# Holding full-array TensorE work back until the next step's projections are placed

## The chip, the cores and the metric

The kernel runs on one core of a Trainium2 chip. The metric is the device time of one execution in microseconds, of which each kernel got several. All executions quoted here ran fast (granted TensorE clock 0.98 to 0.99 over the span).

In the profile's lines PE is TensorE (matmuls), ACT is ScalarE, DVE is VectorE, POOL is GpSimd and SP is SyncE, which issues the DMA transposes. L753 is line 753 of the kernel. An *eviction* is the copy by ACT or DVE that takes a matmul's result out of its accumulator (`pb`) into SBUF. A *landing* is the time from the issue of a transfer to its arrival.

## The reference

Four blocks follow one another, each with a residual and a layernorm: A, B, A, B. Block A is a recurrence of 64 steps ("segments") of 32 tokens with 8 memory tokens. Block B is a linear attention without recurrence.

```python
def _A_ref(x, mem0, Wq, Wk, Wv, Wo, seg_len):   # x 1x2048x512, 32 heads of 128, M = 8, seg_len = 32
    mem = mem0
    for s in range(n_seg):
        h = jnp.concatenate([mem, xs], axis=1)          # xs: the segment's 32 tokens
        q, k, v = (einsum('btd,dhe->bhte', h, W) for W in (Wq, Wk, Wv))
        ...                                             # mask, softmax
        o = jnp.einsum('bhqk,bhke->bhqe', p, v)
        o = jnp.einsum('bhte,hed->btd', o, Wo)
        mem = o[:, :M, :].copy()                        # the next step needs this
        outs.append(o[:, M:, :])
...
x = x + _A_ref(_layernorm(x), ...)
x = x + _B_ref(_layernorm(x), B_wqkv, B_wo)
x = x + _A_ref(_layernorm(x), ...)
x = x + _B_ref(_layernorm(x), B_wqkv, B_wo)
```

The chain from step to step is: memory rows of h, projections, scores and attention of the memory rows, output projection, "next memory" (the selection of the 8 memory rows, transposed), and the projections again.

## The kernel before

The kernel is a program that builds its own instruction order. Each piece of work becomes a node with a cost, an engine, a mode ("col" for TensorE's 32-column tiles, "full" for the whole array) and a priority from the table OFFSET. A list schedule then places the nodes at build time. The token-only part of h (the "left-over" rows, one block of projections for each group of four steps) and block B's work serve as filler beside the recurrence. "x scores" are the attention scores of the token rows, "x sums" the sums of their softmax.

```python
def turned(W, key, blk, bkeys, b, dst, dkey, urgent, dma):   # q or k, half b, turned so that e is on partitions
    tl = project(W, key, blk, bkeys, b, urgent)              # 16 column-tile matmuls of 512 columns
    ...
    nd = evac(img[:, k, :], lambda: tl.f32()[:, :], 512, ...)
    if dma:                                                  # half 0 of q and k, and the left-over block
        add("sp", lambda e: e.dma_start_transpose(dst.rearrange("p h j x -> p h (j x)"), img[:, k, :]), 1.25, ...)
        return nd
    ...                                                      # half 1: 16 transposes on TensorE, then an eviction
def sums(pe):                                                # x sums, full array
    o = tl.f32()[:, 256:512].rearrange("p (h q) -> p h q", h=8)
    pe.matmul(o, bo_sb[:, :], Px[:, :, :], start=True, stop=False)
    return pe.matmul(o[:, :, 0:8], bo_sb[:, :], PLL[:, g2, :, gl], start=False, stop=True)
def next_mem(s, w):                                          # full array, one matmul for each half
    ...
            return pe.matmul(tl.f32()[:, 16 * h:16 * h + 16], outW[:, w, 128 * h:128 * h + 128], selm_sb[:, :],
                             start=True, stop=True)
        add("pe", mm, 0.13, reads=[("outW", w, h), "selm"], tiles=[tl], urgent=True)
...
for i in range(4):                                           # output weights in four parts
    ... s.dma_start(Wo_sb[:, hs, :], wo_view[:, hs, :]) ... after=[late[-2]]
    late.append(nd)
```

`late` holds the weight loads in order, so the second part of Wo waits for Wv, the third for the first part, the fourth for the second.

The softmax here doesn't subtract the row's maximum and nothing guards it: scores larger than these inputs give would overflow.

Of the kernel before, what the change touches and what calls it, by code (L numbers as in the profile page):

```python
# [18 lines left out]
TURN = 1.8  # L19
MODE_SLACK = 13.03  # L20

LOOK = 0.073

PERIOD = 13.5
OFFSET = {
    "ld0": (0.05,),
    "ld1": (7.40,),
    "ld2": (2.50,),
    "ld3": (-5.00,),
    "ld4": (0.50,),  # L30
    "startF": (-0.15,),
    "prepF": (9.60, 3.45, -2.05, 2.25, -11.65, 7.20, 10.15, 0.00, 0.25, -2.25, 10.95),
    "left0F": (-6.25, -5.55, -4.70, 8.10, 1.10, 5.50),
    "left1F": (-3.35, 2.30, 1.95, 0.40, 0.00, 0.00),
    "leftv0F": (10.40, -13.80),
    "leftv1F": (-3.30, 4.80),
    "leftsF": (18.35, 1.45, 0.00, 1.00),
    "xl": (-5.85,),
    "qk0": (-12.95, -6.45, 8.05, -4.60, -13.05, 0.00),
    "qk1": (-0.20, 0.35, 5.25, -8.40, 2.50, -2.40, 9.25, -8.65),  # L40
    "v0": (-0.55, -0.90),
    "v1": (8.80, -1.35),
    "mem0": (0.00, -13.00, -2.00, -17.55, -26.85, -27.15, -14.75, -2.10, -0.90),
    "mem1": (4.25, 0.00, -7.80, -23.75, -16.20, 5.95, 6.50, -7.85, -17.95),
    "out": (2.10, -0.45, -23.15, 0.05),
    "next": (-1.20, 7.90, -0.75),
    "x": (7.25, 0.90, 0.00, 9.35, 8.55, -9.50, 8.35, -18.15, -6.05, 43.75, -2.50, 3.20, -4.50, -1.00, 4.50,
        -8.10, 0.00, 20.70, 27.10, -7.10, 25.80, -2.00, 1.60),
    "res": (44.00, 3.50, -3.65, 4.65, -11.50, 0.50, -0.15),
    "prep": (-11.65, -5.70, 0.00, -1.20, -0.30, -4.45, 0.60, -12.75, -15.65, -8.55, -12.05),  # L50
    "left0": (-4.05, 9.15, 3.55, -11.25, -2.45, 3.55),
    "left1": (0.40, 1.35, -3.70, 27.15, 1.10, -1.45),
    "leftv0": (29.25, 0.25),
    "leftv1": (16.10, 3.05),
    "lefts": (12.95, -2.65, 3.45, 0.45),
    "bi": (1.10, -0.95, 2.45, -8.45, -3.70, -13.50, -7.60, -0.80, -0.75, 14.70, 9.05, -1.60, 5.90, -2.85,
        19.95, 3.55, 4.65, -6.75, -1.20, -4.45, -6.25, 13.60, -15.25),
    "xL": (6.15, 14.85, 0.00, -0.65, 8.15, -18.50, 0.00, 16.95, -6.95, 8.65, -10.95, -11.15, -0.50, 7.10, 0.25,
        2.45, 4.85, -3.40, -1.55, 1.25, 0.70, 1.85, -5.55),
    "outL": (2.90, -6.30, 2.15, -13.50),  # L60
    "resL": (3.05, 0.10, 30.35, 1.95, -12.55, 5.05, 2.05),
    "biL": (-10.20, -13.70, -30.55, -9.65, 5.20, -12.00, -1.55, -6.15, 10.10, 2.55, 0.20, 5.15, 23.35, -10.60,
        21.70, 1.35, -2.40, 7.10, -1.40, -11.85, 4.30, 17.05, 4.30),
    "bm": (0.40, -22.15, -6.45, -6.75, -9.40, 14.30, 1.65, -9.70, 10.35, 3.65, -33.85, 15.75, -5.20),
    "boF": (-5.65, 9.70, -18.05, -1.25, 20.15, -8.70, -6.00, 8.15),
    "bo": (4.10, -23.70, 4.30, 5.10, -10.15, -3.90, -2.35, 0.00),
    "boL": (3.10, 0.90, -3.25, 4.45, -6.85, 2.75, -11.45, 28.45, -4.85),
}
# [35 lines left out]
class _Node:  # L104
    __slots__ = ("engs", "fn", "cost", "sync", "order", "tiles", "dsem", "dval", "eng", "start", "done",
                 "tail", "sig", "val", "waits", "know", "idx", "succ", "nleft", "urgent", "mode", "prio", "lat", "soft", "key")


class _Prog:
# [27 lines left out]
    def add(self, engs, fn, cost, reads=(), writes=(), tiles=(), dsem=None, urgent=False, mode="full",  # L137
# [3 lines left out]
        nd.lat = lat  # L141
        nd.key = None
        if self.place is not None:
            step, name = self.place
            nd.key = (step, name, self.count)
            self.count += 1
# [43 lines left out]
    def schedule(self):  # L190
# [90 lines left out]
        EPS = 0.03  # L281

        def pick_for(e):
            tn = self.now[e]
# [6 lines left out]
            while ready[e]:  # L291
                item = heapq.heappop(ready[e])
                nd = item[2]
                if nd.done is not None:
                    continue
                if first_of(nd):
# [34 lines left out]
        while n_left:  # L331
# [7 lines left out]
            if pick is None:  # L339
                ev = [t for t in self.now.values() if t > t_low + 1e-9]  # L340
                for e in ENGINES:
                    if pend[e]:
                        ev.append(pend[e][0][0])
                for own in self.bank_owner:
                    if own is not None and own.ops[-1].done is not None:
                        ev.append(own.ops[-1].done + PE_LAG)
                        ev.append(own.ops[-1].done + HOP)
                nxt = [t for t in ev if t > t_low + 1e-9]
                if not nxt:
                    raise RuntimeError("scheduler stuck: %d left" % n_left)  # L350
                t = min(nxt)
                for e in ENGINES:
                    if self.now[e] < t:
                        self.now[e] = t
                continue
# [19 lines left out]
            if e == "pe":  # L375
                if nd.mode != self.pe_mode:
                    nd.start += PE_SWITCH
                self.pe_mode = nd.mode
            nd.done = nd.start + nd.cost[e] + nd.lat
            self.now[e] = nd.start + nd.cost[e] - (0.09 if e == "act" else 0.05 if e == "dve" else 0.0)  # L380
# [94 lines left out]
def _build_kernel(nc, A_x, A_mem0, A_Wq, A_Wk, A_Wv, A_Wo, A_seg_len, B_wqkv, B_wo, out):  # L475
# [144 lines left out]
    late = []  # L620
    for i, (W, v, nm, t) in enumerate(((Wq_sb, qk_view[0], "Wq", 12.4), (Wk_sb, qk_view[1], "Wk", 22.0),
                                       (Wv_sb, qk_view[2], "Wv", 31.0))):
        P.at(-9000 + 1000 * i, "ld%d" % (2 + i))
# [3 lines left out]
    for i in range(4):  # L627
        hs = slice(8 * i, 8 * i + 8)
        nd = add("sp", lambda s, hs=hs: s.dma_start(Wo_sb[:, hs, :], wo_view[:, hs, :]), 0.9, writes=[("Wo", i)],
                 dsem="dWo%d" % i, after=[late[-2]], lat=(12.4, 5.6, 5.7, 5.8)[i])  # L630
        late.append(nd)
    add("sp", lambda s: s.dma_start(wqkv_sb[:, :, :], B_wqkv.rearrange("(c p) f -> p c f", p=128)), 0.5,
        writes=["wqkv"], dsem="dwqkv", after=[late[-1]], lat=5.0)
    late.append(P.nodes[-1])
# [103 lines left out]
    def a_layer(base, first):  # L738
        def at(s, name):

            P.at(base + s, name + ("F" if s < 0 else "L" if s >= NSEG or (s == NSEG - 1 and name == "x") else ""))


        def project(W, key, blk, bkeys, b, urgent):
            tl = P.tile()
            for c in range(4):
# [3 lines left out]
                def mm(pe, c=c):  # L750
# [4 lines left out]
                    return r  # L755
                add("pe", mm, c_pe4(4, 512), reads=[key] + bkeys, tiles=[tl], urgent=urgent, mode="col")
            return tl
# [25 lines left out]
        def left_block(G, step):  # L783
# [3 lines left out]
            for b in range(2):  # L787
                at(step, "left%d" % b)
                hs = slice(4 * b, 4 * b + 4)
                turned(Wq_sb, "Wq", blk, bk, b, qTl[:, r2, hs, :, :], ("qTl", r2, b), False, True)  # L790
                turned(Wk_sb, "Wk", blk, bk, b, kTl[:, r2, hs, :, :], ("kTl", r2, b), False, True)
            for b in range(2):
# [83 lines left out]
        def x_attention(s):  # L876
# [25 lines left out]
            def sums(pe):  # L902
                o = tl.f32()[:, 256:512].rearrange("p (h q) -> p h q", h=8)
                pe.matmul(o, bo_sb[:, :], Px[:, :, :], start=True, stop=False)
                return pe.matmul(o[:, :, 0:8], bo_sb[:, :], PLL[:, g2, :, gl], start=False, stop=True)
            add("pe", sums, c_pe(1, 256) + c_pe(1, 64), reads=["Px", ("PLL", g2), "bo"], tiles=[tl])
            add("act", lambda a: a.activation(Rx[:, :, :].rearrange("p h q -> p (h q)"), tl.f32()[:, 256:512], ACTF.Ln),
# [29 lines left out]

        def out_proj(oT, keys, urgent):

# [3 lines left out]
            for hh in range(8):  # L943
# [3 lines left out]
                def mm(pe, hh=hh):  # L947
# [7 lines left out]
                    return r  # L955
                add("pe", mm, 2 * c_pe4(4, 256), reads=[("Wo", i) for i in range(4)] + keys[hh // 4], tiles=[tl],
                    urgent=urgent, mode="col")
            for h in range(2):
# [5 lines left out]
        def out_block(s):  # L964
            at(s, "out")
            keys = [[("oTm", s % NO, b), ("oTx", s % NO, b)] for b in range(2)]
            return out_proj(oTb[:, s % NO, :, :], keys, True)

        def next_mem(s, w):
# [3 lines left out]
            for h in range(2):  # L973
                def mm(pe, h=h):
                    return pe.matmul(tl.f32()[:, 16 * h:16 * h + 16], outW[:, w, 128 * h:128 * h + 128], selm_sb[:, :],  # L975
                                     start=True, stop=True)
                add("pe", mm, 0.13, reads=[("outW", w, h), "selm"], tiles=[tl], urgent=True)
            evac(hT[:, G1 % 2, g1, :, 0:8].rearrange("p (d h) m -> p h d m", d=2),
# [53 lines left out]
        for s in range(NSEG):  # L1032
# [6 lines left out]
            for b in range(2):  # L1039
                at(s, "qk%d" % b)  # L1040
                hs = slice(4 * b, 4 * b + 4)
                turned(Wq_sb, "Wq", blk, bk, b, qT[:, r2, hs, :, :], ("qT", r2, b), True, QDMA[b])
                turned(Wk_sb, "Wk", blk, bk, b, kT[:, r2, hs, :, :], ("kT", r2, b), True, KDMA[b])
            for b in range(2):
# [206 lines left out]
```

## Time and profile before

| | us |
|---|---|
| median of 3 runs (range) | 1869.79 (1865.63 to 1869.96) |
| span of the profiled run | 1867.5 |
| first next memory | 60.7 |
| 62 steps of layer 1 / of layer 2 | 831.3 / 841.5 |
| jump between the layers / tail | 67.5 / 66.6 |

The table's cut at the first matmul of next memory in each step is the prediction's. The page's views are read in the prediction. It uses PE's wait list only in part, so here are its first rows for 56 steps of layer 1 (100 to 860 us). A row gives the waiting line, what ended the wait, the total in us, the number of waits and the longest.

```profile
PE pb L775 <- ACT arena_sb L591: 4.6, 7, 1.2
PE pb L803 <- DMA arena_sb<-arena_sb: 2.6, 3, 0.9
PE pb L775 <- DVE arena_sb L592: 2.5, 4, 1.0
PE pb L753 <- DVE arena_sb L592: 2.3, 14, 0.2
PE pb L837 <- DMA arena_sb<-arena_sb: 1.4, 3, 0.8
```

### The profile page before, as it was taken

How to read it: one execution, taken by the hardware profiler on the slowest of the kernel's cores; microseconds unless marked ns; L12 is line 12 of the kernel's file. 1: busy time of each engine (PE TensorE's matmuls, PEld its weight loads, DVE VectorE, ACT ScalarE, POOL GpSimd, SP SyncE). 2: the span in 40 equal slices, each digit the busy share in tenths (PEclk: the TensorE clock that was granted, in tenths of full speed). 3: DMA queues.
4: the chain of work that ended last, by engine and by line, in shares of the span. 5: the costliest groups of instructions: out<-in, count | busy, mean ns of one | idle time of the engine just before them, and what ended most of it. 6: DMA issues, size and time to landing. Idle time of an engine off the chain costs nothing.

```text
span 1867.5 us, 95161 instructions
## 1 busy us (share of the span) xinstructions
PE 1762.9 (94%) x43796; PEld 1201.8 (64%) x43905; DVE 1065.5 (57%) x3267; ACT 1160.3 (62%) x3015; POOL 74.5 (4%) x172
## 2 busy tenths in 40 slices
PE   4899999999999999999799999999999999999996
PEld 1566767666666667676456666766667666676662
DVE  1455555656565565655445556556555665565555
ACT  2466666666666666666456666666666666666655
POOL 2000000000000000000000000000000000000000
PEclk8999999999999999999899999999999999999999
DMA  9512121221222121211021222122122221212213
GB/s 336 126 35 42 35 43 37 43 40 37 43 37 43 35 46 37 45 38 40 21 42 35 42 38 48 40 37 45 37 44 42 45 43 38 45 38 54 45 34 124
DMA packets 228256, 96.86 MB, mean 52 GB/s; under 512 B 211624, under 2 KB 222000, under 8 KB 226320
## 3 DMA queue, kind: packets, MB, share of 16 engines
q1 hardware_dynamic: 220656, 62.58, 18.1%
q0 software_dynamic: 5616, 15.60, 2.7%
q10 hardware_dynamic: 1584, 12.58, 1.7%
q8 instruction: 343, 5.62, 1.3%
q14 instruction: 57, 0.47, 0.1%
HBM read 29.89 MB, written 10.49 MB: 22 GB/s over the span
## 4 chain that ended last, share of the span: by engine, by line
PE 85%; DMA 10%; ACT 2%; DVE 2%; issue 1%; SPq 0%; ACTq 0%; DVEq 0%
PE pb L753 39%; PE pb L952 15%; DMA arena_sb<-arena_sb 8%; PE pb L928 4%; PE pb L837 3%; PE pb L775 3%; PE pb L993 3%; PE pb L1088 2%; PE pb L975 2%; PE pb L854 2%; PE pb L892 2%; PE pb L1124 1%; PE pb L868 1%; PE pb L1190 1%; PE pb L867 1%
## 5 line engine op out<-in xcount | busy, mean ns | idle before, releaser
L591 ACT ACTIVATE arena_sb<-pb 128x512 bf16<-128x512 f32 (+6 forms) x1309 | 682.0, 530 | 341.5 <-PE pb L753 272.5
L753 PE MATMUL pb<-Wk_sb,arena_sb 128*32 128x512 bf16 x5120 | 347.7, 383 | 5.5 <-DMA Wk_sb<-in_A_Wk_dram 5.5
L753 PE MATMUL pb<-Wv_sb,arena_sb 128*32 128x512 bf16 x5120 | 352.2, 381 | 0.0
L753 PE MATMUL pb<-Wq_sb,arena_sb 128*32 128x512 bf16 x5120 | 342.2, 383 | 5.4 <-DVE arena_sb L592 4.8
L952 PE MATMUL pb<-Wo_sb,arena_sb 128*32 128x256 bf16 x10368 | 312.3, 275 | 4.9 <-DMA Wo_sb<-in_A_Wo_dram 2.9
L592 DVE CAST arena_sb<-pb 128x128 bf16<-128x128 f32 (+3 forms) x452 | 179.9, 398 | 221.3 <-PE pb L975 110.0
L952 PEld LDWEIGHTS pb<-Wo_sb,arena_sb 128*32 128x32 bf16 x10368 | 274.2, 97 | 20.7 <-DMA Wo_sb<-in_A_Wo_dram 3.4
L913 DVE TENSOR_TENSOR arena_sb<-arena_sb 32x256 bf16<-32x256 bf16 x512 | 212.1, 414 | 50.9 <-ACT arena_sb L909 38.8
L592 DVE COPY arena_sb<-pb 128x512 bf16<-128x512 bf16 (+2 forms) x325 | 121.2, 380 | 191.6 <-PE pb L775 183.9
L753 PEld LDWEIGHTS pb<-Wk_sb,arena_sb 128*32 128x32 bf16 x5120 | 136.9, 97 | 133.6 <-DMA Wk_sb<-in_A_Wk_dram 5.6
L753 PEld LDWEIGHTS pb<-Wq_sb,arena_sb 128*32 128x32 bf16 x5120 | 124.2, 96 | 111.3 <-DVE arena_sb L592 10.6
L753 PEld LDWEIGHTS pb<-Wv_sb,arena_sb 128*32 128x32 bf16 x5120 | 132.5, 97 | 98.1 <-issue 2.8
L591 ACT ACTIVATE outW_sb<-pb 128x128 fp32r<-128x128 f32 x228 | 63.2, 277 | 200.0 <-PE pb L952 198.0
L775 PEld LDWEIGHTS pb<-id_sb,arena_sb 128*32 128x32 bf16 x4096 | 76.4, 96 | 95.0 <-ACT arena_sb L591 47.5
L775 PE MATMUL pb<-id_sb,arena_sb 128*32 128x128 bf16 x4096 | 103.1, 220 | 24.1 <-ACT arena_sb L591 20.2
L928 PE MATMUL pb<-arena_sb 128*128 128x128 bf16 x1024 | 118.7, 217 | 5.5 <-DVE arena_sb L915 5.5
L592 DVE CAST outW_sb<-pb 128x128 fp32r<-128x128 f32 x96 | 28.0, 292 | 161.6 <-ACT outW_sb L591 161.6
L915 DVE TENSOR_TENSOR arena_sb<-arena_sb 32x64 bf16<-32x64 bf16 x512 | 110.8, 216 | 15.7
L844 ACT ACTIVATE arena_sb<-pb 128x256 bf16<-128x256 f32 x252 | 92.1, 383 | 41.1 <-PE pb L837 33.1
L929 PE MATMUL pb<-arena_sb 128*128 128x32 bf16 x1024 | 109.7, 178 | 0.0
L928 PEld LDWEIGHTS pb<-arena_sb 128*128 128x128 bf16 x1024 | 87.8, 96 | 7.2 <-DVE arena_sb L915 5.9
L837 PE MATMUL pb<-arena_sb 128*128 128x32 bf16 x2016 | 89.3, 177 | 2.8 <-DMA arena_sb<-arena_sb 2.5
(109 smaller groups left out, 2270.2 us busy)
## 6 DMA issues: line engine op xcount, KB each, us to landing
arena_sb<-arena_sb SPq DMA_TRANSPOSE x384, 2.5
Wq_sb<-in_A_Wq_dram ACTq DMA_DIRECT2D x1, 4096.0 KB, 13.5
Wk_sb<-in_A_Wk_dram ACTq DMA_DIRECT2D x1, 4096.0 KB, 23.7
Wv_sb<-in_A_Wv_dram ACTq DMA_DIRECT2D x1, 4096.0 KB, 34.4
Wo_sb<-in_A_Wo_dram SPq DMA_DIRECT2D x4, 1024.0 KB, 7.5
xs_scratch<-x_sb POOLq DMA_DIRECT2D x32, 128.0 KB, 2.0
pq_scratch<-arena_sb POOLq DMA_DIRECT2D x32, 128.0 KB, 2.5
x_sb<-xs_scratch POOLq DMA_DIRECT2D x16, 128.0 KB, 2.3
```

The lines of the kernel that those rows point to most:

```text
L591: return e.activation(o() if callable(o) else o, i() if callable(i) else i, ACTF.Copy)
L592: return e.tensor_copy(o() if callable(o) else o, i() if callable(i) else i)
L753: r = pe.matmul(tl.f32()[32 * j:32 * j + 32, 0:512], blk[:, c, :], W[:, c, o:o + 512], start=(c == 0), stop=(c == 3), tile_position=(0, 32 ...
L775: r = pe.transpose(tt.bf16()[32 * j:32 * j + 32, 128 * i:128 * i + 128], img[:, k, o:o + 32], id_sb[:, :], tile_position=(0, 32 * j))
L837: r = pe.matmul(tl.f32()[:, o:o + 32], kk[:, hh, :, :].rearrange("p j x -> p (j x)"), qT[:, r2, hh, :, 0:8], start=True, stop=True)
L844: add("act", lambda a: a.activation(Pm[:, k, :, :].rearrange("p a q -> p (a q)"), tl.f32()[:, 0:256], ACTF.Exp, scale=SCALE), c_act(256), ...
L913: add("dve", lambda v, q=q, j=j: v.tensor_tensor(Pbx[q, :, j, 0:32], Px[q, :, :], Rx[q, :, :], ALU.mult), c_dve(256) + 0.075, reads=["Px", ...
L915: add("dve", lambda v, q=q, j=j: v.tensor_tensor(Pbx[q, :, j, 32:40], PLL[q, g2, :, gl], Rx[q, :, 0:8], ALU.mult), c_dve(64) + 0.075, read ...
L928: pe.matmul(o, vimg[:, r2, e], Pbx[:, hh, :, 0:32], start=True, stop=False)
L929: return pe.matmul(o[:, :, 0:8], vleft[:, g2, e], Pbx[:, hh, :, 32:40], start=False, stop=True)
L952: r = pe.matmul(tl.f32()[32 * j:32 * j + 32, 0:256], oT[:, 4 * hh + n, :], Wo_sb[:, 8 * n + hh, 256 * d:256 * d + 256], start=(hh == 0 and ...
L993: r = pe.matmul(tl.f32()[:, 256 * d:256 * d + 256], sel(d), outW[:, u, :], start=first and d == 0, stop=last, skip_group_check=True)
```

## The change

The intent: in each step TensorE changes between column tiles and full array four times. If next memory and x sums also run in column tiles, and no full-array node is placed between the output projection and the next step's six projections, one pair of changes should go. Apart from that, two parts of the output weights are loaded right after Wk, and step 0 turns q and k on TensorE, to begin the recurrence sooner. The priority table was tuned anew for this.

```diff
-MODE_SLACK = 13.03
-LOOK = 0.073
+MODE_SLACK = 6.37
+LOOK = 0.000
 OFFSET = {                       # all some 300 priorities new (cut), step 0 has its own
...
+                if e == "pe" and gate[0] > 0 and nd.mode == "full":
+                    kept.append(item)
+                    continue
...
+                if nd.gate:
+                    gate[0] = nd.gate if nd.gate > 0 else gate[0] - 1
...
-                 dsem="dWo%d" % i, after=[late[-2]], lat=(12.4, 5.6, 5.7, 5.8)[i])
-        late.append(nd)
+                 dsem="dWo%d" % i, after=[late[1 + i // 2]], lat=(12.5, 14.5, 7.3, 9.8)[i])
...
+            if urgent:
+                nd.gate = -1                     # each of the six projections of a step
...
-                turned(Wq_sb, "Wq", blk, bk, b, qTl[:, r2, hs, :, :], ("qTl", r2, b), False, True)
+                turned(Wq_sb, "Wq", blk, bk, b, qTl[:, r2, hs, :, :], ("qTl", r2, b), False, step > 0)
...                                              # x sums: the same two sums as four column tiles each
+                            pe.matmul(o, bo_sb[:, q], Px[:, :, :], start=True, stop=False, tile_position=(0, 32 * j))
...
+                if hh == 0 and more:
+                    nd.gate = 6                  # first matmul node of an output projection
...
-                    return pe.matmul(tl.f32()[:, 16 * h:16 * h + 16], outW[:, w, 128 * h:128 * h + 128], selm_sb[:, :],
-                                     start=True, stop=True)
-                add("pe", mm, 0.13, reads=[("outW", w, h), "selm"], tiles=[tl], urgent=True)
+                    for j in range(4):
+                        o = 128 * h + 32 * j
+                        r = pe.matmul(tl.f32()[32 * j:32 * j + 32, 16 * h:16 * h + 16], outW[:, w, o:o + 32].bitcast(F32),
+                                      selm_sb[:, :].bitcast(F32), start=True, stop=True, tile_position=(0, 32 * j))
+                    return r
+                add("pe", mm, 0.075, reads=[("outW", w, h), "selm"], tiles=[tl], urgent=True, mode="col")
...
-                turned(Wq_sb, "Wq", blk, bk, b, qT[:, r2, hs, :, :], ("qT", r2, b), True, QDMA[b])
+                turned(Wq_sb, "Wq", blk, bk, b, qT[:, r2, hs, :, :], ("qT", r2, b), True, QDMA[b] and s > 0)
```

Lines move: of the lines named below, 753 becomes 774 (projections), 775 becomes 798 (transposes on TensorE), 803 becomes 826 (left-over scores), 837 becomes 860 (memory scores), 952 becomes 982 (output projection), 975 becomes 1009 (next memory), 904 and 905 become 934 and 931 (x sums).

## The prediction

> **What bounds the kernel now.** I read three things in this order: the page's summary and slices, the PE rows in order of time in one steady step, and the chain of waits during the start. The page:
>
> ```profile
> PE 1762.9 (94%) x43796; PEld 1201.8 (64%) x43905; DVE 1065.5 (57%) x3267; ACT 1160.3 (62%) x3015; POOL 74.5 (4%) x172
> ...
> PE   4899999999999999999799999999999999999996
> ...
> PEclk8999999999999999999899999999999999999999
> ...
> PE 85%; DMA 10%; ACT 2%; DVE 2%; issue 1%; SPq 0%; ACTq 0%; DVEq 0%
> ```
>
> TensorE is busy in every slice but the first two, one in the middle (between the two recurrent layers) and the last; DVE and ACT are near 60%; PE is 85% of the chain that ended last. So in the steady part only TensorE time counts, and at the start something else does.
>
> To cut the span up, I took the first start of the next-memory matmul (line 975) in each recurrent step. There are 126 such steps: the first at 60.7 us, a jump of 67.5 us between the layers (891.9 to 959.5), the last at 1801.0, then 66.6 us to the end. The 124 intervals inside the layers sum to 831.3 + 841.5 = 1672.8 us, mean 13.49. That gives 60.7 + 1672.8 + 67.5 + 66.6 = 1867.6, the span. Any gain must come out of one of these four terms.
>
> Inside a step, the PE rows in order of time show this:
>
> ```profile
> 311.33 0.71 PE L952 MATMUL pb<-Wo_sb,arena_sb 128*32 128x256 bf16 x17
> 311.85 0.40 PE L753 MATMUL pb<-Wk_sb,arena_sb 128*32 128x512 bf16 x4
> 312.07 0.62 PE L753 MATMUL pb<-Wv_sb,arena_sb 128*32 128x512 bf16 x8
> 312.62 0.28 PE L975 MATMUL pb<-selm_sb,outW_sb 128*128 128x16 f32 x1
> 312.75 0.28 PE L904 MATMUL pb<-arena_sb,bo_sb 128*128 128x256 bf16 x1
> 312.87 0.19 PE L905 MATMUL pb<-arena_sb,bo_sb 128*128 128x64 bf16 x1
> 312.90 0.26 PE L975 MATMUL pb<-selm_sb,outW_sb 128*128 128x16 f32 x1
> 313.08 0.62 PE L753 MATMUL pb<-Wv_sb,arena_sb 128*32 128x512 bf16 x8
> 313.53 0.39 PE L753 MATMUL pb<-Wq_sb,arena_sb 128*32 128x512 bf16 x4
> ```
>
> The weights' shape gives the mode: 128\*32 is a column tile, 128\*128 the full array. The output projection (952) is in column tiles; then the kernel fills with left-over V projections, switches to the full array for next memory (975) and x sums (904, 905), and switches back. Starts, not durations, carry the cost, since matmuls overlap. A second pair of switches surrounds the memory attention, later in the step.
>
> The start: PE waits for the last part of the output weights.
>
> ```profile
> 42.11 6.86 DMA Wo_sb<-in_A_Wo_dram
> 48.97 0.02 issue
> 48.99 8.13 DMA Wo_sb<-in_A_Wo_dram
> 57.12 0.04 issue
> 57.16 2.90 PE pb L952 x64
> ```
>
> The second part of Wo was only issued at 42.11, although its condition (Wv landed at 36.22) was met six microseconds before: SyncE was occupied by three DMA transposes from 34.28 for 7.78 us. The first output projection starts at 57.16, 0.04 us after the fourth part landed.
>
> **What the skill says.** *TensorEngine Tiling (Array Packing)*, Key Properties: changing the tiling mode drains TensorE. The trace agrees and gives a size. From one matmul's start to the next, medians over 100 to 860 us: projection to next memory 309 ns against 206 for projection to another column-tile line (+103); transpose (775) to memory scores (837) 152 against 47 (+105); 905 to projection 122 against 28 to a full-array matmul (+94); 868 to projection 106 against 25 (+81). In that stretch there are 113 switches into full mode and 113 back for 56 steps: two pairs a step, about 97 ns a switch. *TensorE: Matmul & The Clock Gate*, Back-to-back issue gap: about N/2.4 + 2.5 ns for an isolated warm matmul. The trace has 215 ns for 512 columns on the full array, and about 215 for four column tiles of 512 together, so column tiles cost the same stream time per quad. The same page, Part 1, says that an idle array falls to half clock; the chip's clock line agrees: granted clock 0.64 to 0.65 from 24 to 48 us, where PE waits for weights. *FP8 and Floating Point Precision*, TensorE Precision Notes: true FP32 takes four passes. No run here yet shows an FP32 column tile.
>
> **The change, part by part.**
>
> 1. *The gate.* From the first matmul of an output projection until the six projections of the next step (q, k, v, two halves each) are placed, no full-array node is picked. Residual (993), second-block (1088, 1100, 1124) and memory work moves behind the projections, beside the memory attention, which is full-array anyway. With next memory and x sums turned into column tiles nothing in the gated stretch needs the full array. One pair of switches of the two goes: 2 x 97 = **0.195 us a step**.
>
> 2. *Next memory.* Two 128x16 fp32r matmuls at 133 ns each (975 to 975, median) become two groups of four FP32 column-tile matmuls. The four passes are only over 16 columns and 32-column weights. The change charges 0.075 us a group where the old charged 0.13, and the old charge agrees with the trace's 133. I take 0.075 as an estimate: 2 x (0.133 - 0.075) = **0.11 us a step**. This is my least certain term: it could be 0.
>
> 3. *x sums.* 256 + 64 columns on the full array took 119 + 28 ns from start to start. Four tiles of the same widths stream for the same time (the quad rule above; 256-column quads of line 952 take about 105 ns). **0**, apart from the switches.
>
> 4. *Filler.* Between the output projection's end (311.8) and the next step's first projection (313.53) lies a chain: eviction of two halves on ACT and DVE (0.28 + 0.29), next memory, another eviction (0.19), each with its hop. It is some 1.7 us, less some 0.2 without the switches and with the faster matmul. Allowed filler is column work: left-over projections (6 x 0.86 us per four steps = 1.29 a step), x scores (0.24), x sums (0.15) and the left-over output projection (1.7 per four steps = 0.43), 2.1 us a step against some 1.4 needed. After the projections, full work is 3.3 us a step, against a latency of memory attention of about 3.1 us (307.0 to 310.1). Both fit, with little to spare. I charge nothing in the middle and let the range carry it.
>
> 5. *Start.* Wo parts 0 and 1 are issued after Wk (24.95), parts 2 and 3 after Wv; step 0 and the first left-over block turn q and k on PE, so SyncE has no transposes to stand behind. The before trace moved Wv and the first part, 5 MB, between 24.96 and 39.66. With Wo always queued, the remaining 3 MB at the 217 to 249 GB/s of the windows 36 to 48 and 48 to 57 would take 12 to 14 us from a full queue, less what part 1 already takes beside Wv: landing at 47 to 50. The four V projections after Wv at half clock (4 x 1.7 = 7 us from 36.2) and the memory attention end at about 46 to 47, so Wo still sets it. The first output projection moves from 57.2 to about 48: **9 us**, once.
>
> 6. *Layer boundary and end.* Step 0 of the second layer also turns on PE, where PE has idle time; a DMA turn has a 2.5 us median against under 1.5 us via PE and an eviction. I give it **1 us**; the end 0.
>
> Sum: 124 x (0.195 + 0.11) = 37.8, plus 9, plus 1 = 47.8. From 1869.8 that is **1822 us**, 2.6% faster. The step mean goes from 13.49 to about 13.19.
>
> **Rivals.**
>
> *Switches go, idle comes.* If the static order lacks column filler at the right time (left-over projections are only ready after the layernorm of the next group), PE waits for the eviction chain instead. For it: fill is already tight, and the old kernel used full-array work there in every step. Against: 2.1 us available for 1.4. With 0.2 us idle a step the total is 1847, "same".
>
> *The transposes' jitter is the real floor.* PE waits at 775 for evictions that wait for a DMA transpose to free an image buffer; in the first layer starts 0.8 to 1.5 us late come every few steps (some 17 us in all), and in the second layer every fourth step often takes 14.3 to 15.3 us. The change leaves this in place. If the switching time were partly hidden in these waits, I lose perhaps a fifth: 1830.
>
> *Only the start gains.* If FP32 column tiles cost as much as the full-array form or more, (2) is 0 and the total is 1836, within 2%. *The start gains nothing*, because small Wo rows keep the queues slow: 1831.
>
> *An engine becomes the bound:* ACT and DVE are at 62% and 57%; ruled out.
>
> **Range and chances.** 2% faster is 1832.4, so the centre passes by 10 us. Terms (2) and (5) each have a half-width near 8 to 10 us, idle after the gate perhaps 10, and a denser order could gain 10 more than I count. Range **1804 to 1842**. Chances: faster **0.73**, same **0.26**, slower **0.01**.
>
> **What would show it.** Switches: 113 pairs in 56 steps fall to about 56 to 60 pairs; if there are over 80, step 1 failed. Next memory: starts of its groups some 75 ns apart rather than 133. PE's wait list: no new row for next memory or its projections above some 5 us per layer; if there is, the filler rival held. First output projection near 48 us; first next memory near 51. Step mean near 13.19, jump between layers about 66.5, tail 66 to 67. I am wrong if the step mean stays above 13.3, or if the first output projection stays after 54.

## More of the kernel before

TensorE waits little, and what it waits for is rare and long: 3 to 7 waits of about 1 us in 56 steps.

The page's list of DMA issues has the transposes that stand behind the rare waits; the last number is the median from issue to landing.

```profile
arena_sb<-arena_sb SPq DMA_TRANSPOSE x384, 2.5
```

## The result and the profile after

The changed kernel took 1892.56 us (median of 4 runs, 1887.56 to 1895.94) against 1869.28 (4 runs, 1865.63 to 1869.96) in the same rounds. The ratio is 1.0126, 95% interval 1.0098 to 1.0155: slower by 1.3%, which at a limit of 2% counts as the same. Here and below, a ratio is the mean time of one kernel's fast runs over that of the other's in the same rounds, so it is not quite the ratio of the quoted medians. The prediction had 1822.

| us | before | after | difference |
|---|---|---|---|
| first next memory | 60.7 | 52.0 | -8.6 |
| 62 steps of layer 1 | 831.3 | 853.8 | +22.5 |
| jump between the layers | 67.5 | 59.4 | -8.1 |
| 62 steps of layer 2 | 841.5 | 856.6 | +15.1 |
| tail | 66.6 | 63.9 | -2.7 |
| span | 1867.5 | 1885.8 | +18.3 |
| mode changes in a step | 4.0 | 3.0 | |

Everything that happens once became faster, and the steps became slower by 37.6 us. The page after:

```profile
PE 1757.9 (93%) x46549; PEld 1212.4 (64%) x46629; DVE 1069.5 (57%) x3224; ACT 1174.0 (62%) x3070; POOL 74.8 (4%) x172
...
PE   5899999999999999999799999999999999999996
...
PE 73%; DMA 19%; DVE 4%; ACT 3%; issue 1%; SPq 0%; ACTq 0%; DVEq 0%
...
arena_sb<-arena_sb SPq DMA_TRANSPOSE x372, 2.6
```

The busy shares barely moved: 93% for PE after 94%. The line that moved is the chain: DMA went from 10% to 19% of it, PE from 85% to 73%. PE's wait list for the same 100 to 860 us shows two kinds of wait:

```profile
PE pb L860 <- DMA arena_sb<-arena_sb: 8.7, 16, 1.1
PE pb L798 <- ACT arena_sb L613: 5.0, 11, 0.8
PE pb L774 <- DVE arena_sb L614: 4.0, 13, 0.3
PE pb L1009 <- ACT outW_sb L613: 3.6, 14, 0.4
PE pb L798 <- DVE arena_sb L614: 2.8, 9, 1.0
PE pb L826 <- DMA arena_sb<-arena_sb: 2.3, 4, 0.9
```

The third and fourth row are regular: 13 and 14 times in 56 steps, once in each group of four. The timeline of PE shows one of them (start, length, line, and in brackets the idle time before it and what ended it):

```profile
448.46 1.93 PE L982 MATMUL pb<-Wo_sb,arena_sb 128*32 128x256 bf16 x64
450.21 0.28 PE L934 MATMUL pb<-arena_sb,bo_sb 128*32 128x256 bf16 x4
450.32 0.20 PE L931 MATMUL pb<-arena_sb,bo_sb 128*32 128x64 bf16 x4
450.77 0.58 PE L1009 MATMUL pb<-selm_sb,outW_sb 128*32 128x16 f32 x16 [0.24 <-ACT outW_sb L613]
451.66 1.05 PE L774 MATMUL pb<-Wq_sb,arena_sb 128*32 128x512 bf16 x16 [0.31 <-DVE arena_sb L614]
```

After the output projection only the x sums are left as column work. Next memory starts 0.45 us after the x sums' last group began, and the projections 0.89 us after next memory. The profile counts only 0.24 and 0.31 of this as idle, since it takes the ends of matmuls from a model.

The other rows are irregular, 4 to 16 waits of up to 1.1 us, for DMA transposes or for evictions. The chain of waits shows one such wait:

```profile
539.11 0.04 PE pb L826 x9
539.15 4.13 DMA arena_sb<-arena_sb
543.28 0.05 issue
543.33 0.47 PE pb L860 x12
```

This transpose landed 4.13 us after its issue, where the soonest in this run took 2.4 and the median 2.6, and the memory scores waited for it. In layer 2 the same row of the wait list grew from 0.6 us in total before to 9.7. At the start, the chain's last part of Wo landed at 49.52 and the output projection followed:

```profile
38.98 10.54 DMA Wo_sb<-in_A_Wo_dram
49.52 0.14 issue
49.66 1.06 PE pb L982 x33
```

### The profile page after: what moved, and what is told of

It reads as the page before. It is cut to its first block, busy times and chain, and to the rows that moved or that the text cites. A ratio compares the mean times of both kernels' runs of the same rounds, so it can differ in the third digit from the quotient of the medians.

```text
span 1885.8 us, 100456 instructions
## 1 busy us (share of the span) xinstructions
PE 1757.9 (93%) x46549; PEld 1212.4 (64%) x46629; DVE 1069.5 (57%) x3224; ACT 1174.0 (62%) x3070; POOL 74.8 (4%) x172
## 3 DMA queue, kind: packets, MB, share of 16 engines
q1 hardware_dynamic: 214128, 61.01, 18.2%
## 4 chain that ended last, share of the span: by engine, by line
PE 73%; DMA 19%; DVE 4%; ACT 3%; issue 1%; SPq 0%; ACTq 0%; DVEq 0%
PE pb L774 32%; DMA arena_sb<-arena_sb 15%; PE pb L982 15%; PE pb L958 3%; PE pb L860 3%; PE pb L1123 3%; PE pb L1028 2%; PE pb L798 2%; PE pb L877 2%; PE pb L915 2%; PE pb L890 1%; PE pb L1159 1%; ACT arena_sb L613 1%; PE pb L891 1%; DMA Wk_sb<-in_A_Wk_dram 1%
## 5 line engine op out<-in xcount | busy, mean ns | idle before, releaser
L613 ACT ACTIVATE arena_sb<-pb 128x512 bf16<-128x512 f32 (+6 forms) x1426 | 710.2, 514 | 372.0 <-PE pb L774 269.1
L774 PE MATMUL pb<-Wk_sb,arena_sb 128*32 128x512 bf16 x5120 | 337.5, 381 | 5.6 <-DMA Wk_sb<-in_A_Wk_dram 5.6
L982 PE MATMUL pb<-Wo_sb,arena_sb 128*32 128x256 bf16 x10368 | 325.6, 273 | 4.9 <-DMA Wo_sb<-in_A_Wo_dram 1.2
L614 DVE CAST arena_sb<-pb 128x512 bf16<-128x512 f32 (+3 forms) x421 | 201.2, 478 | 175.1 <-PE pb L774 77.9
L982 PEld LDWEIGHTS pb<-Wo_sb,arena_sb 128*32 128x32 bf16 x10368 | 264.4, 96 | 37.3 <-DVE arena_sb L894 12.1
L613 ACT ACTIVATE outW_sb<-pb 128x128 fp32r<-128x128 f32 x176 | 48.8, 277 | 181.3 <-PE pb L982 179.9
L614 DVE COPY arena_sb<-pb 128x512 bf16<-128x512 bf16 (+2 forms) x251 | 92.2, 368 | 119.6 <-PE pb L798 111.3
L614 DVE CAST outW_sb<-pb 128x128 fp32r<-128x128 f32 x148 | 43.1, 291 | 176.4 <-ACT outW_sb L613 93.3
L798 PE MATMUL pb<-id_sb,arena_sb 128*32 128x128 bf16 x4288 | 109.6, 221 | 14.0 <-ACT arena_sb L613 7.7
L860 PEld LDWEIGHTS pb<-arena_sb 128*128 128x128 bf16 x2016 | 69.0, 96 | 48.4 <-DMA arena_sb<-arena_sb 23.2
## 6 DMA issues: line engine op xcount, KB each, us to landing
Wo_sb<-in_A_Wo_dram SPq DMA_DIRECT2D x4, 1024.0 KB, 11.9
```

The source lines that it names most:

```text
L613: return e.activation(o() if callable(o) else o, i() if callable(i) else i, ACTF.Copy)
L614: return e.tensor_copy(o() if callable(o) else o, i() if callable(i) else i)
L774: r = pe.matmul(tl.f32()[32 * j:32 * j + 32, 0:512], blk[:, c, :], W[:, c, o:o + 512], start=(c == 0), stop=(c == 3), tile_position=(0, 32 ...
L798: r = pe.transpose(tt.bf16()[32 * j:32 * j + 32, 128 * i:128 * i + 128], img[:, k, o:o + 32], id_sb[:, :], tile_position=(0, 32 * j))
L860: r = pe.matmul(tl.f32()[:, o:o + 32], kk[:, hh, :, :].rearrange("p j x -> p (j x)"), qT[:, r2, hh, :, 0:8], start=True, stop=True)
L982: r = pe.matmul(tl.f32()[32 * j:32 * j + 32, 0:256], oT[:, 4 * hh + n, :], Wo_sb[:, 8 * n + hh, 256 * d:256 * d + 256], start=(hh == 0 and ...
```

## The experiments

All runs of one group shared a chip and the runs of the kernel before, whose medians were 1870.18 (e), 1869.84 (p), 1871.71 (f), 1866.48 (c1, c2) and 1868.19 (c3, c4).

### Parts of the change alone

**e1: only the start.** The old order, with the Wo order and the TensorE turns of step 0 and of the first left-over block.

```diff
-                 dsem="dWo%d" % i, after=[late[-2]], lat=(12.4, 5.6, 5.7, 5.8)[i])
+                 dsem="dWo%d" % i, after=[late[1 + i // 2]], lat=(12.5, 14.5, 7.3, 9.8)[i])
-                turned(Wq_sb, ..., ("qT", r2, b), True, QDMA[b])
+                turned(Wq_sb, ..., ("qT", r2, b), True, QDMA[b] and s > 0)
```

> The kernel before with only the start parts of the change: output weights issued behind the key and value weights, and step 0 and the first left-over block turned on TensorE; the priorities of the steps and the steps' plan are those of before. My theory now: the start and the layer boundary are gains by themselves (first next memory 60.7 to about 52, jump between the layers 67.5 to about 59.5), the 124 steps stay at 1673 us: total near 1852, 0.991 of before. Rival: the gain at start and boundary is only work moved into later steps, so the steps grow by as much: total near 1869.

Measured: 1864.75 us, ratio 0.9973 (0.9949 to 0.9998). First next memory came at 52.0 and the jump took 59.0 us, so start and boundary gained the same 17 us as in the changed kernel. The steps lost 10.8 of them again (834.9 + 848.7): in this schedule every later node has its place relative to the start, and the build-time plan itself had already moved by 3.6 us in layer 2. In 56 steps of layer 1 the waits of line 775 for ACT rose from 4.6 to 7.8 us, and over both layers (100 to 860 and 965 to 1720 us) those of lines 803 and 837 for transposes from 6.7 to 11.0; what the rest is stays open.

**e2: only the new forms, in the old order.** Next memory and x sums in column tiles, but given to the schedule with the old cost and mode, so that nothing changes place.

```diff
-                    return pe.matmul(tl.f32()[:, 16 * h:16 * h + 16], outW[:, w, ...], selm_sb[:, :], ...)
+                    for j in range(4):
+                        ... tile_position=(0, 32 * j))
                 add("pe", mm, 0.13, reads=[("outW", w, h), "selm"], tiles=[tl], urgent=True)
```

> The kernel before with its order on every engine kept, instruction for instruction; only next memory and the x sums are issued in column tiles instead of on the full array. My theory now: the forms are worth what I sized or more (next memory 0.267 to some 0.11 to 0.2 us a step, switches 4 to about 3.5 in the first layer and 4 in the second): 0.1 to 0.2 us a step, total 1845 to 1857. Rival: FP32 column tiles cost as much as the full-array form: total within 3 us of before; or the waits eat it: same.

Measured: 1872.43 us, ratio 1.0011 (0.9990 to 1.0032); steps 832.5 + 843.1. A miss: no gain in the total. Mode changes fell from 4.0 to 3.5 a step in layer 1 and not at all in layer 2. Yet the starts show that the forms do save time where they stand: from the last matmul before next memory or x sums to the first one after them, 112 steps took 68.9 us in place of 80.6. Even between a column tile and a full-array matmul, next memory with its mode change took 281 ns in place of 350. Some 12 us were freed, then, and the steps did not become shorter. A good half went into longer waits for transposes, 14.2 us in place of 6.7 at lines 803 and 837 over both layers. The two rows of layer 1, 100 to 860 us, which showed 2.6 and 1.4 before:

```profile
PE pb L803 <- DMA arena_sb<-arena_sb: 4.9, 6, 1.1
PE pb L837 <- DMA arena_sb<-arena_sb: 3.4, 6, 1.0
```

So the rival "the waits eat it" fits better than "the forms cost as much"; one profiled run does not show it for certain.

**e3: forms and start, in the old order.** The two edits above together.

> Both of the last two together, still no gate and the old order of the steps. My theory: the two gains add: 1828 to 1840, so the loss of the whole change lies in the new order (the gate with its priorities) alone. Rival: forms or start bring the loss; then this is no faster than before.

Measured: 1852.78 us, ratio 0.9908 (0.9883 to 0.9934); first next memory 52.2, steps 829.9 + 841.9, jump 60.3. That is less than expected, but it keeps 16 us at start and boundary, and it is the fastest version that is not wrong: it beats both kernels. It also differs from e1 in the forms alone (the two build the same plan), and there the forms were worth 12 us, all of it in the steps (1683.6 down to 1671.8), with no overlap of the two runs' times. The effects of start and forms don't simply add: -5 and +2 us alone, -17 together. Beside the changed kernel it differs in the order alone, and its steps take 38.6 us less. So the loss belongs to the new order (gate and new priorities together), not to the forms.

**e4: the old forms in the new order.** The converse of e2: the changed kernel with full-array next memory and x sums, at the same places.

```diff
+                    return pe.matmul(tl.f32()[:, 16 * h:16 * h + 16], outW[:, w, 128 * h:128 * h + 128], selm_sb[:, :],
+                                     start=True, stop=True)
                 add("pe", mm, 0.075, reads=[("outW", w, h), "selm"], tiles=[tl], urgent=True, mode="col")
```

> The changed kernel with its order kept instruction for instruction, but next memory and the x sums issued on the full array as before. Counted in that order, switches go from 3 to 8 a step (5 x 0.097 = 0.485 us), and next memory costs 0.15 us more: 0.6 us a step if TensorE is never idle around them, less where it is: total 1930 to 1970. If the gap after the output projection were idle in every step, the switches would hide there and the total would stay within 20 us of the changed kernel.

Measured: 1933.82 us, ratio 1.0336 (1.0316 to 1.0355), with 8.0 mode changes a step. As expected: within the new order the forms are needed, and are worth 41 us. By the expectation's own prices (0.63 us a step) it would be 78; the steps took 45 more, so such prices overstate what reaches the total.

### What bounds the steps

**p1 and p3: more TensorE work.** In p1 the kernel before, in p3 the changed one, turns half 1 of k twice on TensorE (expected: about 0.19 us a step more).

```diff
-                for i in range(4):
+                for i in (0, 1, 2, 3) * (2 if urgent and W is Wk_sb else 1):
```

**p2 and p4: a longer recurrence.** On the engine that evicts next memory, a copy of the same size goes first, to an unused buffer (about 0.2 us on the chain from step to step, no TensorE work).

```diff
+            junk = copy(junk_sb[:, :], lambda: tl.f32()[:, 0:32])
+            add(ANY, lambda e: (junk(e), once(e))[1], ...)
```

> The kernel before, order kept; each step turns its second k half on TensorE twice (16 more column-tile matmuls, some 0.19 us, same result). Theory L (the step is a loop whose own latency, through evictions, DMA transposes and softmax, is about as long as TensorE's work, so PE time no longer sets the step): the probe costs well under its 24 us, 0 to 15. Rival P (TensorE time alone sets the step, as my prediction had it): plus 22 to 26 us.

> The kernel before, order kept; the eviction that carries the next memory is preceded by an idle copy of the same 32 columns on the same engine (about 0.2 us of ACT or DVE on the recurrence, no TensorE work). Theory L: plus 12 to 25 us. Rival P: TensorE has other work queued there, so under 6 us.

> The changed kernel, same PE probe as in the first. Theory L, stronger here because the waits have grown: 0 to 12 us over the changed kernel's 1892. Rival P: plus 22 to 26.

> The changed kernel, same loop probe as in the second. Theory L: plus 20 to 26 us over 1892 (the full 0.2 us a step, since in the gated gap nothing covers it). Rival P: under 6.

Measured: p1 1902.20 (ratio 1.0166), p2 1869.36 (0.9997, 0.9980 to 1.0014), p3 1912.39 (1.0228), p4 1901.94 (1.0166). The traces size the doubled turn at 0.22 us a step (330 ns from start to start became 553), 28 us in all rather than the expected 24. So the kernel before paid 32 us for 28 us of TensorE work and nothing for latency: TensorE bounds it, and the chain has some 0.2 us to spare. The changed kernel paid 20 us for the TensorE work and 9 for the latency (against its own 1892.6, from another group; by the ratios to the kernel before, 19 and 7.5): in part of its steps the chain is now on the path. The new order used up the spare time that p2 shows.

**f1 and f2: filling the gap.** The x sums of one step in four run four times, in the changed kernel (f1) and in the one before (f2).

```diff
-                for left in range(2):
+                for left in (0, 1) * (PROBE if g == 1 else 1):     # PROBE = 4
```

> The changed kernel, order kept; in every fourth step (the second of each group of four, 31 or 32 a layer) the x sums are done four times instead of once, same result: 3 x 0.137 = 0.41 us more TensorE work. In the first layer they stand directly before next memory, where the trace shows TensorE waiting 0.41 us (436 ns from start to start where 28 would do) for the output's eviction. Theory (the gated gap is empty in that step, so the gate exposes the eviction chain): free in the first layer, below 5 us in all. Rival (the gap is not what bounds the step): plus 13 us per layer, 20 to 26 in all.

> The kernel before with the same probe, order kept (full-array form, 3 x 0.147 = 0.44 us). There the gap holds x sums and second-block work and TensorE is busy in it, so it should cost its full time: 64 x 0.44 = 28 us, 20 to 32. If it were free here too, the gap in the changed kernel would not be the difference.

The expectation's count was wrong: one step in four is 32 steps in all, so the full cost is 32 x 0.41 = 13 us in f1 and 32 x 0.44 = 14 in f2. Measured: f2 1885.57, 14 us over the kernel before, the full cost; its gap has no room. f1 1906.18, 13.6 us over the changed kernel (10 by the ratios), which looks like most or all of the full cost too. But its trace shows that the wait of line 1009 for ACT vanished from the list, as it does when the gap had been empty, while waits for transposes grew a little there (line 860 from 8.7 to 9.1 us, line 826 from 2.3 to 4.1; these are the changed kernel's line numbers) and in layer 2 (line 860 from 9.7 to 11.9). One cost may have hidden the other: f1 is inconclusive alone. It raised the question of the next group.

### The DMA transposes

**c1, c2 and c4: plain copies in place of the DMA transposes**, in the changed kernel (c1), in e3 (c2) and in the kernel before (c4). Order, waits and all other instructions stay.

```diff
-                add("sp", lambda e: e.dma_start_transpose(dst.rearrange("p h j x -> p h (j x)"), img[:, k, :]), 1.25,
+                add("sp", lambda e: e.dma_start(dst.rearrange("p h j x -> p (h j x)"), img[:, k, :]), 1.25,
```

These kernels are wrong on purpose: the scores of half of the heads and of the left-over rows are computed from tiles that were not turned. The comparison with the reference passed nevertheless, so it doesn't notice these scores.

> The changed kernel with every DMA transpose of the steps replaced by a plain DMA copy of the same tile between the same two SBUF tensors. The result is wrong on purpose; order, waits and all other instructions stay. A copy should land sooner and more evenly than the transpose's median of 3.08 us (half of them over 3.05). Theory L (late landings are what the new order loses on): the waits of memory scores and left scores on these transfers, 0.06 to 0.16 us a step in layer 1 and up to 0.25 in layer 2, go, and with them what they push back: the 124 steps fall from 853.8 + 856.6 to about 830 + 842, no more than 5 us above the same copy version of the old order with the new forms and start. Theory G (the chain output projection, eviction, next memory, eviction, projection has no column work to fill it): these waits on ACT and DVE stay, the steps fall by 10 to 20 us at most, and the copy version of the old order stays 20 us or more ahead.

> The old order with the new forms and the new start, with the same replacement of the DMA transposes by plain copies (result wrong on purpose). Its steps take 829.9 + 841.9 us with transposes. Theory L: both orders are freed of late landings, this one gains 5 to 15 us and the difference between the two orders shrinks from 38.6 us to under 10. Theory G: the difference stays at 20 us or more.

> The kernel before with its DMA transposes replaced by plain copies (result wrong on purpose). Steps 831.3 + 841.5 with transposes; the old order with the new forms and plain copies took 814.7 + 832.7, the changed kernel with plain copies 821.1 + 836.4. If the new forms are worth what the prediction gave them (0.11 us a step for next memory, and part of the switches in this order) and only the transposes hid it, this kernel stays at 826 or above in layer 1 and 840 or above in layer 2, 18 us or more above the same order with the new forms. If the forms are worth nothing with transposes out of the way either, it falls to 816 and 834.

| steps, layer 1 + layer 2, us | transposes | copies | gained |
|---|---|---|---|
| before | 831.3 + 841.5 = 1672.8 | 817.7 + 831.5 = 1649.2 | 23.6 |
| old order, new forms and start (e3, c2) | 829.9 + 841.9 = 1671.8 | 814.7 + 832.7 = 1647.4 | 24.4 |
| changed kernel | 853.8 + 856.6 = 1710.4 | 821.1 + 836.4 = 1657.5 | 52.9 |

The times: c1 1832.12 (ratio 0.9813, 0.9795 to 0.9831), c2 1824.39 (0.9770), c4 1837.51 (0.9841). Between the new and the old order with the same forms and start, 38.6 us of steps became 10.1: 28.5 us, three quarters, were the transposes. Neither theory's numbers were met: L wanted a rest of 5 us or less (under 10 in c2's expectation), G one of 20 or more. The rest of 10.1 us is what the order costs by itself, its gap less the mode changes that it saves.

A copy differs from a transpose in more than lateness, so "late" is not shown apart from "long": the soonest landing was 1.93 us in place of 2.39, and SyncE issued the next one after 0.86 us in place of 1.23 where two stood close together. In layer 1 of the changed kernel 48% of the transposes, but 13% of the copies, landed after more than 3.05 us, which is what the plan allows for one (1.25 to issue and 1.8 more).

PE's wait list of c1, 100 to 860 us:

```profile
PE pb L774 <- DVE arena_sb L614: 4.1, 13, 0.3
PE pb L1009 <- ACT outW_sb L613: 3.8, 15, 0.4
PE pb L798 <- ACT arena_sb L613: 0.6, 1, 0.6
```

Of the irregular rows one wait is left. Those that the profile put down to ACT and DVE at line 798 are gone too, which fits evictions that had waited in turn for an image buffer that a transpose still read. The two regular rows stand as they were. On c1's page, the share of the chain and the landing of the copies:

```profile
PE 90%; DMA 4%; DVE 3%; ACT 2%; issue 1%; SPq 0%; ACTq 0%; DVEq 0%
...
arena_sb<-arena_sb SPq DMA_DIRECT2D x372, 128.0 KB, 2.0
```

In the same stretch of c4 the list has two rows in all:

```profile
PE pb L753 <- DVE arena_sb L592: 2.3, 14, 0.2
PE pb L775 <- DVE arena_sb L592: 0.9, 2, 0.6
```

c4 also bears on the forms: beside c2 its steps take 1.8 us more. That is little, but the two ran on different chips, on which the kernel before differed by 1.7 us, and c2's plan (e3's) is 3.6 us longer in layer 2 than c4's. The record thus has 0 us for the forms (e2), 12 (e3 beside e1) and 2 to 5 (c2 beside c4), against 12 by the starts. What they are worth in the old order is not settled.

**c3: a smaller x load.** In layer 1 the changed kernel issues the x load of the next group 3.04 us into the second step of each group of four, between that step's two transposes (2.61 and 3.85); the kernel before issued it 7.11 us into the first, when both had landed. c3 loads 8 rows in place of 128 from the fourth group on (wrong result).

```diff
-                x_move(x_sb[:, slot(t), :], x_view[t], slot(t), [], [("x", slot(t))], "dxl")
+                rows = 128 if t < NX else 8
+                x_move(x_sb[0:rows, slot(t), :], x_view[t][0:rows], slot(t), [], [("x", slot(t))], "dxl")
```

> The changed kernel with the x load of each group of four steps in layer 1 cut from 128 rows to 8 from the fourth group on (result wrong on purpose); same order, same waits. In the changed kernel this load is issued 3.04 us into the second step of each group, between the step's two DMA transposes at 2.61 and 3.85, and the first of these lands after 3.55 us in every such step instead of 2.4; the fastest of these steps takes 13.25 us, 12.77 with plain copies. In the kernel before it is issued 7.11 us into the first step, when both transposes have landed. Theory X (this collision is a fixed part of what the order loses): those transposes land after 2.4 to 2.5 us, the fastest of these steps falls to about 12.8, and layer 1 falls by 16 times 0.48 = 8 us to about 846; layer 2, which has no such load, stays at 855 to 858. Rival: the transposes are late there whatever else moves; layer 1 stays above 850.

Measured: 1889.84 (1886.13 to 1893.34), ratio 1.0112 (1.0082 to 1.0142); layer 1 852.1, layer 2 863.0. In these 16 steps the first transpose landed after a median of 3.02 us instead of 3.59, not the 2.4 to 2.5 expected; the fastest affected step fell from 13.25 to 12.77 us, and the mean of all 16 from 13.51 to 13.17, which is 16 x 0.34 = 5 us. But layer 1 as a whole fell by 1.7 us only, and layer 2, where nothing was changed, rose by 6.4. The collision is real and small; in the total it is lost in the spread that late landings give this kernel. Most of the lateness is of another origin: in layer 1 still 45% of the transposes landed after more than 3.05 us, against 48%.

## Why the prediction was wrong

The steps' +37.6 us of the profiled runs split into three terms. Only the third is measured by an experiment; the first is an estimate from starts, and the second is the remainder.

- **The gain at the prices of the starts: -30.2 us, an estimate.** Mode changes fell from 4 to 3 a step: 124 x 0.097 = 12.0. A half of next memory (four FP32 column-tile matmuls in the code, eight records in the trace) takes 60 ns to the next matmul where the full-array one took 133, so next memory costs 0.12 in place of 0.267 us: 124 x 0.147 = 18.2. e4 shows that not all of such a sum need reach the total.
- **The gap: +38.5 us**, about 0.31 a step. It is the remainder that brings -30.2 to the +8.3 us between the copy versions of the kernels before and after. The start-to-start distances agree in layer 1: in c1 they hold some 0.3 us a step more of waits before projections, next memory and output projection than in c4.
- **The transposes: +29.3 us**, the difference of what copies gain in the changed kernel (52.9) and in the one before (23.6).

The kernels' own build-time plan agrees with the first two. Built again from both kernels, without a run, it gives the 124 steps 828.7 + 841.4 us before and 829.5 + 840.6 after: no gain at all. It saves the mode changes and the matmul time, but TensorE's idle time in these steps rises from 16.5 to 44.8 us, 34 of it before next memory and the first q and k projections. So the gap stood in the plan before anything ran, and the prediction did not look there.

Against the prediction's own steps:

1. *The gate* failed by half. There are 84 pairs of changes in 56 steps, over the 80 that the prediction named as failure. A layernorm transpose runs on the full array between the V projections and the turn of k, and left-over projections and x scores break the full-array stretch once more. Worth 12 us, not 24.
2. *Next memory*, called the least certain term, was right and a little small: 0.147 us a step against 0.11. The chain of waits shows such a group between output matmuls of the changed kernel:

```profile
548.51 0.46 PE pb L982 x15
548.97 0.06 PE pb L1009 x7
549.03 0.22 PE pb L982 x7
```

3. *x sums*: right; from their start to the next matmul of the same mode 138 ns in column tiles (changed kernel), 147 on the full array (before).
4. *Filler* is the step that failed most. "I charge nothing in the middle and let the range carry it" was a term of about 0.31 us a step. The sum of filler over four steps was enough, as reckoned, but it isn't there at the right time: the left-over output projection is used up in one step of four, the left-over projections are not ready until two steps later, and in between the x sums alone cover a chain of evictions. The kernel before filled that place with full-array work of the second block, which the gate forbids. The average was checked where each single step had to be. The rival *switches go, idle comes* described this and put 0.2 us on it. The step mean came to 13.79 us in place of 13.19. The sign that the prediction had set, a new row above some 5 us in PE's wait list, did not show it: the two rows stood at 4.0 and 3.6 us, as the list counts only part of these waits.
5. *Start*: right; the output projection started at 49.66 for "about 48", and next memory came 8.6 us sooner for 9.
6. *Boundary and end* were too small: 8.1 and 2.7 us for 1 and 0. e1 and e3 have the boundary's gain (8.5 and 7.2) without the new order, so it comes from the TensorE turns of step 0 and of the first left-over block.

The rival *the transposes' jitter is the real floor* was given "perhaps a fifth" of the gain. It was worth 29 us, about as much as the whole estimated gain of the steps. The error was to take the jitter as a fixed sum that the change leaves in place. It is not: putting copies in place of the transposes gained 24 us in the one order and 53 in the other.

One reading of the prediction is loose though little rests on it: granted clock 0.64 to 0.65 "from 24 to 48 us, where PE waits for weights". In the same view PE was busy for 9.96 of the 12 us from 36 to 48, and the clock was 1.00 from 48 to 57 with PE busy for 5.25 of 9. The clock does not simply follow the idle time of its own window.

What stays open: why the transposes cost more in the new order. Two things are seen and not told apart. They land later (mean in layer 1 3.13 us against 2.92 in e3, 48% over 3.05 us against 36%; copies 2.32 against 2.26), for which the x load accounts in one step of four at most. And a wait now meets a TensorE with less other work ready. The gate and the new priorities could not be separated either: the build-time plan falls apart without the gate (around 15 changes a step with the new priorities), and the gate with the old priorities was not run, so the loss is the order's as a whole. The split into terms rests on one profiled run of each kernel, the changed kernel's runs spread by 8 us, and its profiled run was the fastest of its four.

## What to carry to other kernels

Before taking work out of the place where it fills a gap, list what can fill the gap in each single step of the pattern; a sum over the period proves nothing about the step that has none. Where a program places its own instructions at build time, read the idle time of that plan first. When the bounding engine also shows rare, long waits for transfers, measure their price first, for instance by putting a faster transfer of the same size in their place: here the transposes held 24 us of the kernel before, more than any correct edit tried here was worth. And a change of several independent parts should be tried part by part: start and forms without the new order were 0.9% faster while the whole was 1.3% slower.

## What the Trainium skill lacked or had wrong

- *Advanced Engine Details and Errata*, X-Bar Transpose (TRN2), says that transpose DMAs are as fast as regular ones. Here a transpose from SBUF to SBUF took a median of 2.5 us from issue to landing, and over 3.05 us in 34% of the cases (before, layer 1); a plain copy of the same tile between the same buffers took 1.97, and over 3.05 in 11%. Copies in place of the transposes were worth 24 to 53 us of a kernel of 1870.
- No page has the spread of single transfers. Transposes here landed after 2.4 to 4.9 us (before, layer 1), and a load of 128 rows issued between two of them put the first at a median of 3.59 us, where it took 3.02 with a load of 8 rows.
- *TensorEngine Tiling (Array Packing)*, Key Properties, says that a change of mode drains TensorE and gives no size: about 97 ns here.
- No page has the cost of FP32 matmuls in column tiles: the four for a half of next memory (16 columns each) took 60 ns to the next matmul here, the fp32r form on the full array 133.
